# Turning the planes of the normalized rows by transposing DMAs from SBUF to SBUF

## The chip, the core and the metric

The kernel runs on one core of one Trainium2 chip. Its time is the device time of one launch in microseconds (us). Before the change three runs took 516.69, 516.65 and 516.27 us; the median is 516.65. A profiled execution of the same kernel took 516.58 us.

The names of the engines: PE is TensorE's matmuls and PEld its weight loads, DVE is VectorE, ACT is ScalarE, POOL is GpSimd, and SP is SyncE, which issues all DMAs here. SBUF is the memory on the core with 128 partitions, PSUM the memory into which PE writes, and DRAM is the chip's main memory.

## The reference

A causal attention over a window of 64 positions is followed by a mixture layer with SoLU and a layer norm:

```python
scores = scale * np.matmul(q, k.transpose(0, 1, 3, 2))      # B, H, S, D = 8, 8, 576, 64
mask = (rel >= 0) & (rel < 64)                              # rel = query - key position
scores = np.where(mask, scores, -1e9)
attn = np.exp(scores - scores.max(-1)); attn = attn / (attn.sum(-1) + 1e-09)
x = (attn @ v).transpose(0, 2, 1, 3).reshape(4608, 512)
h = x @ w_in                                                # 512 x 1024
sm = softmax of h over the row (with 1e-9 in the sum)
solu = h * sm
ln = (solu - mean) / np.sqrt(var + 1e-06) * g_ln
y = ln @ w_out                                              # 1024 x 512, float32
```

## The kernel before, in words

The 4608 tokens are 36 tiles of 128 (NTILE). For each tile the work has these parts, named after the functions that plan them:

- `load` fetches queries and keys (`qk`, L457) and values (`v`, L459). `scores` (PE, L499) and `softmax` (DVE L513 to L552, ACT L536, POOL) make the attention weights `sS`.
- From tile 8 on, POOL copies the 16-bit halves of `sS` into a buffer `raw` (L572); one DMA stores them to DRAM (`pd`, L580) and one transposing DMA brings them back into `raw` turned (L583). There are 28 such tiles. For the first eight tiles PE transposes `sS`.
- `values` (PE, L630) multiplies the turned weights with the values. ACT and DVE split the result into `xH` and `xL` (DVE L641).
- `moe_in` (PE, L669, and L658 for the first three tiles) multiplies with `w_in`, as three passes over high and low parts, into `pH`: 24 matmuls.
- `moe_norm` makes `e`, the normalized rows of 1024 values: a maximum (DVE L684), exponential (ACT L686), the product with h (DVE L689), small statistics on DVE (L692 to L703), a square (ACT L695), a power on POOL (L702), and the normalization (L708, on POOL or DVE).
- `planes` writes each normalized row as two 16-bit floats, a high plane (L736, mostly ACT) and a low plane (L739, mostly DVE; on POOL for the first tiles). The buffer `pl` is 128 x 2 x 1024, f16, 512 KB a tile.
- `turn` brings both planes into `yT`, with the 1024 features across partitions, as 8 groups of 128. This is done by DMA for tiles 1 to 33, 33 in all; the others are transposed by PE.
- `moe_out` (PE, L802) multiplies `yT` with `w_outH` and `w_outL`: 24 matmuls a tile (high x high, high x low, low x high). ACT scales the result to `ot` (L813), and a DMA stores it (L817).

The loop is a software pipeline. In turn t stand, in this order, `turn(t-1)`, `moe_in(t)` with `moe_norm` and `planes`, `values(t+1)`, the attention of a tile some four ahead, and `moe_out(t-3)`.

The weights are prepared within the first tiles. `weight_block(i)` takes raw 64-bit weights (blocks 0 to 3 are `w_in`, 4 to 7 `w_out`): POOL takes the low bits (L364), DVE joins them (L368, L371, L373). `split` then makes the high parts of `w_in` (L427), the low parts `w_8` to `w_11` (L429), and, scaled by `gs_sb`, `w_outH` (L434) and `w_outL` (L436).

What sets the order: each operation goes to a `Plan` with an engine, an estimated cost, what it reads and what it writes. `Plan.order` gives each one a due time by going back from PE's order, and then lists them: of the operations that are ready on the engine that is free first, the one with the earliest due time comes next. A table `HOMES` puts single tasks on engines, and `RINGS` says how many buffers each name has. SP is one queue in this plan. Where the plan foresees PE waiting in the first stage, it puts in filler matmuls on the identity (`pO_filler`, L911). On the chip each engine works through its list in that order and waits for semaphores.

Of the kernel before, what the change touches and what calls it, by code (L numbers as in the profile page):

```python
# [14 lines left out]
U16 = mybir.dt.uint16  # L15
# [5 lines left out]
P = 128  # L21
# [14 lines left out]
FURTHER = 4  # L36

HASTE = 1

LOOSE = 2  # L40
BEHIND = 3
# [45 lines left out]

RINGS = {
# [3 lines left out]
}  # L92

# [1 line left out]
class Plan:  # L95
# [62 lines left out]
    def order(self):  # L158
        n = len(self.ops)
        before = self.edges()  # L160
        after = [[] for _ in range(n)]
        for i, b in enumerate(before):
            for j, whole in b.items():
                after[j].append((i, whole))
        left = [len(b) for b in before]
        topo = [i for i in range(n) if not left[i]]
        for j in topo:
            for i, _ in after[j]:
                left[i] -= 1
                if not left[i]:  # L170
                    topo.append(i)
        assert len(topo) == n, "the rings are too small for this order"

        clock, due = 0, [1e9] * n
        for i, o in enumerate(self.ops):
            if o[0] == "PE":
                due[i] = clock
                clock += 0 if o[6] else o[1]
        for j in reversed(topo):
            for i, whole in after[j]:  # L180
                lat = self.ops[j][5] if self.ops[i][0] != self.ops[j][0] or self.ops[i][0] == "SP" else 0
                due[j] = min(due[j], due[i] - (HASTE * (self.ops[j][1] + lat) if whole else 0))
        left = [len(b) for b in before]
        ready = [0] * n
        free = dict.fromkeys(("PE", "DVE", "ACT", "POOL", "SP"), 0)
        waiting = {e: set() for e in free}
        for i in range(n):
            if not left[i]:
                waiting[self.ops[i][0]].add(i)
        out, moved, shown = [], 0, False  # L190
        while any(waiting.values()):

            begin, e = min(
                (max(free[e], min(ready[i] for i in w)), e) for e, w in waiting.items() if w)
            i = min((i for i in waiting[e] if ready[i] <= begin), key=lambda i: (due[i], i))
            waiting[e].remove(i)
            if e == "PE" and not shown:
                shown = any(k[0] == "pO" for k in self.ops[i][4])
                n = 0 if shown else int((begin - max(free[e], self.FILL_FROM)) * self.FILL // self.FILL_COST)
                if n > 0:  # L200
                    out.append(self.filler(n))
            out.append(self.ops[i][2])
            end = begin + self.ops[i][1]
            free[e] = end
            if e == "SP":
                free[e] = begin + (1900 if self.ops[i][1] == 2600 else 480)
                moved = end = max(moved, begin) + self.ops[i][1]
            for j, whole in after[i]:
                if whole:
                    ready[j] = max(ready[j], end + (self.ops[i][5] if self.ops[j][0] != e or e == "SP" else 0 if e == "PE" else 90))  # L210
                else:
                    ready[j] = max(ready[j], begin)
                left[j] -= 1
                if not left[j]:
                    waiting[self.ops[j][0]].add(j)
        self.span = max(free.values())
        return out
# [3 lines left out]
def tile_window_attention_solu_moe(  # L221
# [17 lines left out]
    nc = tc.nc  # L239
# [4 lines left out]
    DFF = w_in.shape[1] // 2  # L244
# [3 lines left out]
    NF = DFF // P  # L248
# [6 lines left out]
    dr = ctx.enter_context(tc.tile_pool(name="dr", bufs=3, space=bass.MemoryType.DRAM))  # L255
# [33 lines left out]
    for first in (0, None, 1):  # L289
        t = masks[first] = const.tile([P, P], F32, name=f"mask{first}")  # L290
# [27 lines left out]
    plan = Plan(RINGS)  # L318

    def T(tag, n, shape, dtype=F32, pool=None):  # L320

        if (tag, n) not in plan.tiles:
            plan.tiles[tag, n] = (pool or sb).tile(
                shape, dtype, tag=tag, name=f"{tag}_{n}", bufs=RINGS[tag])
        return plan.tiles[tag, n]

    def W32(i):
        return T("w", i, [P, 2, 512])
# [383 lines left out]
    def crosses(t):  # L712

        return BY_DMA[0] <= t < NTILE - BY_DMA[1]

    def PL(t):
        return T("pl", t, [P, 2, DFF], F16)

    def YD(t):
        return T("yd", t, [2 * P, DFF], U16, pool=dr)  # L720

    def YT(t):
        return T("yF" if t < PLAIN_OUT else "yT", t, [P, NF, P])

    def Y(t, k):

        return YT(t).rearrange("p a b -> p (a b)").bitcast(F16).rearrange(
            "p (a k b) -> p a k b", a=NF, k=2)[:, :, k]
# [13 lines left out]
    def turn(t):  # L742
        if not crosses(t):
            return
        plan.dma(P * DFF * 4, lambda: nc.sync.dma_start(
            YD(t).rearrange("(k p) n -> p k n", k=2), PL(t).bitcast(U16)),
            [("pl", t, h) for h in range(2)] + [("pl", t, h, 1) for h in range(2)], [("yd", t)], 3500)
        plan.op("SP", 2600, lambda: nc.sync.dma_start_transpose(
            YT(t).rearrange("p a b -> p (a b)").bitcast(U16).rearrange("p (a b) -> p a b", a=NF), YD(t)),
            [("yd", t)], [("yT", t)], 2000)  # L750

    def moe_transpose(t):
        if crosses(t):
# [27 lines left out]
    def moe_out(t):  # L781
        last = t == NTILE - 1
        bank = ("pX", NTILE) if last else ("pO", t)

        def PO():
            if last:
                return T(*bank, [P, NC, P], pool=ps_x).rearrange("p a b -> p (a b)")
            return T(*bank, [P, DM], pool=ps_o)

        if t < PLAIN_OUT:  # L790
            for f in range(NF):
                plan.op("PE", 930, lambda f=f: nc.tensor.matmul(  # L792
                    PO(), YT(t)[:, f], W32(NC + f // 2)[:, f % 2],
                    start=(f == 0), stop=(f == NF - 1)),
                    [("yF", t, f), ("w", NC + f // 2)], [bank])
        for f in range(NF if t >= PLAIN_OUT else 0):
            i, x = NC + f // 2, f % 2
            high, low = ([("yT", t)],) * 2 if crosses(t) else (
                [("yT", t, f // 4)], [("yT", t, f // 4, 1)])
            for k, (y, w, keys) in enumerate((  # L800
                    (0, WH, high + [("H", i, x)]), (0, WL, high + [("L", i, x)]), (1, WH, low + [("H", i, x)]))):
                plan.op("PE", 216, lambda f=f, i=i, x=x, k=k, y=y, w=w: nc.tensor.matmul(  # L802
                    PO(), Y(t, y)[:, f], w(i, x), start=(f == k == 0), stop=(f == NF - 1 and k == 2)),
                    keys, [bank])

        def ot():
            return T("ot", t, [P, DM])

        parts = ((slice(0, DM // 2), "ACT", 330), (slice(DM // 2, DM), "DVE", 350)) if last else (
            (slice(0, DM), "ACT", 580),)  # L810
        for x, (cs, e, cost) in enumerate(parts):
            by = 1 / Y_SCALE if t < PLAIN_OUT else unscale
            plan.op(e, cost, lambda cs=cs, e=e, by=by: nc.scalar.mul(  # L813
                ot()[:, cs], PO()[:, cs], by) if e == "ACT" else nc.vector.tensor_scalar(
                ot()[:, cs], PO()[:, cs], by, 0.0, ALU.mult, ALU.add),
                [bank] + [("inv",)] * (t >= PLAIN_OUT), [("ot", t, x)])
            plan.dma(P * DM * 4 // len(parts), lambda cs=cs: nc.sync.dma_start(  # L817
                out[t * P:(t + 1) * P, cs], ot()[:, cs]), [("ot", t, x)], [])
# [43 lines left out]
    for t in range(NTILE + BEHIND):  # L862
        for a in ahead(t):
            on(load, a + 1)
        on(turn, t - 1)
        if t == PLAIN_IN:
            for i in range(NC):
# [13 lines left out]
        else:  # L881
# [16 lines left out]
            if t - BEHIND + 1 >= NTILE - BY_DMA[1]:  # L898
                on(moe_transpose, t - BEHIND + 1)
            on(moe_out, t - BEHIND)  # L900
            if (t, 1) == SCALED:
                out_scale()
# [58 lines left out]
```

## Time and profile before

| what | value |
|---|---|
| median of three runs | 516.65 us |
| profiled execution, whole | 516.58 us |
| its span, first to last instruction | 514.8 us |
| mean granted TensorE clock | 0.996 |
| DMA traffic | 115.57 MB, mean 225 GB/s |
| stores of the planes `yd<-pl` | 33 of 512 KB |
| transposes `yT<-yd` | 33 |

The profile gives busy time by engine, the chain of work that ended last, groups of instructions by line, and rows of a timeline. A row of the chain has start, length and work, all in us. A row of the timeline has start, busy length, engine, line, operation, result and sources by the program's names, shapes and a count; brackets hold the idle time ahead of it and what ended that. A row of the DMA issues has the count, the KB of each and the median us from issue to landing. A row for a stretch of time has its length and the busy time of PE, PEld, DVE, ACT and POOL with counts, the granted clock, the busy share of the DMA engines, and GB/s.

### The profile page before, as it was taken

Reading aid. Unit: us, or ns where it says so; the run is one execution under the profiler, and the core shown is the slowest. Engines: PE = TensorE matmul, PEld = TensorE weight load, DVE = VectorE, ACT = ScalarE, POOL = GpSimd, SP = SyncE. Lnnn points to the kernel's source line nnn. Section 1 sums busy time; section 2 is a strip of 40 time slices with the busy share of each in tenths; the row PEclk is TensorE's granted clock in tenths of the full one; section 3 lists DMA queues with packets and bytes.
Section 4 is the critical chain, followed back from the end, with each engine's and each line's share of the span. In section 5 each row is a group of like instructions: output and inputs, shape, how many; then the busy total and the mean of one; then the engine's idle time right before and its main releaser. Section 6 shows DMA issues by size and latency. Waiting matters only on the chain.

```text
span 514.8 us, 11432 instructions
## 1 busy us (share of the span) xinstructions
PE 503.9 (98%) x4222; PEld 335.7 (65%) x4222; DVE 362.6 (70%) x677; ACT 338.9 (66%) x978; POOL 261.7 (51%) x459
## 2 busy tenths in 40 slices
PE   8899799999999999999999999999999999999997
PEld 7555576666666666666666666666666666666653
DVE  4999997987666777777777777777777777754330
ACT  5577777768866666666666666666666666673240
POOL 5726662457366555555555555555555555571110
PEclk9999999999999999999999999999999999999999
DMA  8992124769899999999999999999999997799201
GB/s 347 415 373 73 52 55 140 212 188 255 234 245 269 260 230 307 253 239 227 272 230 275 235 259 278 268 254 243 253 243 249 295 270 213 183 216 202 85 36 47
DMA packets 157448, 115.57 MB, mean 225 GB/s; under 512 B 129872, under 2 KB 130128, under 8 KB 156880
## 3 DMA queue, kind: packets, MB, share of 16 engines
q1 hardware_dynamic: 157392, 114.84, 81.9%
q8 instruction: 33, 0.54, 0.4%
q14 instruction: 23, 0.19, 0.1%
HBM read 41.42 MB, written 41.42 MB: 161 GB/s over the span
## 4 chain that ended last, share of the span: by engine, by line
PE 90%; DVE 7%; DMA 1%; issue 1%; ACT 1%; DVEq 0%; ACTq 0%
PE pH L669 36%; PE pO L802 35%; PE pX L630 7%; PE pS L499 6%; PE pH L658 2%; DVE w L371 1%; PE pO L792 1%; DVE w L373 1%; DVE w L368 1%; PE pX L802 1%; DVE sS L552 1%; PE t L606 1%; DMA qk<-qk 1%; DVE nmx L520 1%; PE t L764 1%
## 5 line engine op out<-in xcount | busy, mean ns | idle before, releaser
L802 PE MATMUL pO<-w_outH,yT 128*128 128x512 f16 x544 | 167.7, 380 | 0.0
L802 PEld LDWEIGHTS <-yT 128*128 128x128 f16 x840 | 79.6, 98 | 96.6 <-issue 5.1
L552 POOL TENSOR_SCALAR sS<-sS,rec 128x128 f32<-128x128 f32 x240 | 92.4, 406 | 69.1 <-DVE rec L548 64.8
L669 PE MATMUL pH<-w_inH,xH 128*128 128x512 f32 x264 | 111.0, 421 | 3.3 <-DVE mst L689 3.3
L536 ACT ACTIVATE sS<-sS,nmx 128x128 f32<-128x128 f32 x264 | 102.0, 388 | 6.4 <-DVE nmx L513 4.7
L669 PE MATMUL pH<-w_inH,xL 128*128 128x512 f32 x264 | 104.3, 395 | 0.0
L802 PE MATMUL pO<-w_outL,yT 128*128 128x512 f16 x272 | 103.1, 379 | 0.0
L669 PE MATMUL pH<-w,xH 128*128 128x512 f32 x264 | 101.6, 389 | 0.0
L702 POOL TENSOR_TENSOR mst<-mst,neghalf 128x1 f32<-128x1 f32 x36 | 20.8, 579 | 132.0 <-DVE mst L700 130.0
L684 DVE TENSOR_REDUCE mst<-pH 128x1 f32<-128x1024 f32 x36 | 44.0, 1224 | 56.9 <-PE pH L669 55.8
L739 DVE TENSOR_TENSOR pl<-e,pl 128x512 f16<-128x512 f32 x59 | 78.2, 1328 | 3.4 <-ACT pl L736 3.3
L813 ACT ACTIVATE ot<-pO,bound 128x512 f32<-128x512 f32 x34 | 23.4, 688 | 80.1 <-PE pO L802 71.1
L686 ACT ACTIVATE e<-pH,mst 128x1024 f32<-128x1024 f32 x36 | 40.1, 1114 | 32.4 <-DVE mst L684 30.5
L669 PEld LDWEIGHTS pH<-w_inH,xH 128*128 128x128 f32 x264 | 50.2, 190 | 16.1 <-ACT w_inH L427 3.4
L708 POOL TENSOR_SCALAR e<-e,mst 128x512 f32<-128x512 f32 x66 | 51.0, 781 | 18.3 <-DVE mst L703 16.3
L669 PEld LDWEIGHTS pH<-w_inH,xL 128*128 128x128 f32 x264 | 49.9, 189 | 11.9 <-DVE xL L641 0.3
L669 PEld LDWEIGHTS pH<-w,xH 128*128 128x128 f32 x264 | 49.7, 188 | 10.3
L572 POOL COPY raw<-sS 128x1024 uint16<-128x1024 uint16 x52 | 53.0, 1049 | 0.9 <-DVE sS L552 0.9
L695 ACT ACTIVATE unread<-e,mst 128x1024 bf16<-128x1024 f32 x36 | 41.3, 1149 | 16.5 <-DVE mst L693 11.9
L536 ACT ACTIVATION_READ_ACCUMULATOR sS<-sS,nmx 128x1 f32 x264 | 49.6, 188 | 0.0
L689 DVE CUSTOM_DVE_ANT_0 e<-pH,e 128x1024 f32<-128x1024 f32 x36 | 43.8, 1216 | 2.5 <-ACT e L686 2.5
L499 PE MATMUL pS<-qk 64*64 64x128 f32 x1152 | 39.8, 276 | 0.1
(117 smaller groups left out, 706.9 us busy)
## 6 DMA issues: line engine op xcount, KB each, us to landing
qk<-qk SPq DMA_DIRECT2D x36, 640.0 KB, 6.4
yd<-pl SPq DMA_DIRECT2D x33, 512.0 KB, 5.8
pd<-raw SPq DMA_DIRECT2D x28, 512.0 KB, 7.2
v<-vS SPq DMA_DIRECT2D x36, 256.0 KB, 3.6
y<-ot SPq DMA_DIRECT2D x35, 256.0 KB, 6.8
raw<-w_in SPq DMA_DIRECT2D x4, 1024.0 KB, 10.7
raw<-w_out SPq DMA_DIRECT2D x4, 1024.0 KB, 9.0
yT<-yd SPq DMA_TRANSPOSE x33, 5.4
```

Source lines behind the costliest of these rows:

```text
L499: nc.tensor.matmul(PS(t)[half * WIN:(half + 1) * WIN, r, p], q[rs, p, half * WIN:(half + 1) * WIN], keys, start=t not in MASKED, stop=t no ...
L536: plan.op("ACT", 580, lambda h=h: nc.scalar.activation(SS(t)[:, h], PS(t)[:, h // NPAIR, h % NPAIR] if t in MASKED else SS(t)[:, h], AF.Ex ...
L552: SS(t)[:, h], SS(t)[:, h], rec()[:, h:h + 1]) if e == "ACT" else units[e].tensor_scalar(
L572: plan.op(e, {"POOL": 1050, "ACT": 1000, "DVE": 700}[e], lambda x=x, e=e: copy_on(e)(PP(t)[:, :, 4 * x:4 * x + 4].rearrange("p k h n -> p ...
L669: plan.op("PE", 233, lambda n=n, c=c, x=x, w=w: nc.tensor.matmul(PH(t)[:, hs], x(t)[:, c], w(c, h), start=(n == 0), stop=(n == len(passes) ...
L684: plan.op("DVE", 1230, lambda: nc.vector.tensor_reduce(nmax(), PH(t), axis=AX.X, op=ALU.max, negate=True), [("pH", t)], [key(0)])
L686: plan.op("ACT", 1320, lambda: nc.scalar.activation(E(t), PH(t), AF.Exp, bias=nmax(), scale=1.0, accum_out=se()), [("pH", t), key(0)], H2 ...
L689: plan.op("DVE", 1310, lambda: nc.vector.tensor_tensor_reduce(E(t), PH(t), E(t), scale=1.0, scalar=0.0, op0=ALU.mult, op1=ALU.add, accum_o ...
L695: plan.op("ACT", 1330, lambda: nc.scalar.activation(unread, E(t), AF.Square, bias=nmean(), scale=1.0, accum_out=ss()), H2 + [key(4)], [key ...
L708: plan.op(e, {"POOL": 820, "DVE": 400}[e], lambda h=h, hs=hs, e=e: units[e].tensor_scalar(E(t)[:, hs], E(t)[:, hs], nmean(), kk(), ALU.add ...
L739: plan.op(e, {"POOL": 1450, "DVE": 690}[e], lambda hs=hs, e=e: units[e].tensor_sub(PL(t)[:, 1, hs], E(t)[:, hs], PL(t)[:, 0, hs]), [("e", ...
L802: plan.op("PE", 216, lambda f=f, i=i, x=x, k=k, y=y, w=w: nc.tensor.matmul(PO(), Y(t, y)[:, f], w(i, x), start=(f == k == 0), stop=(f == N ...
```

## The change

`turn` no longer stores the planes to DRAM. It issues two transposing DMAs, one for each plane, which read `pl` in SBUF and write every second 128-column group of `yT`. The DRAM buffer `yd` is gone. Each plane has its own key: the first DMA needs the high plane alone, and in `moe_out` the matmuls with the low plane wait for the second DMA. In the plan a plane's DMA has the cost TURN, and SP is held for 1000 ns by it.

```diff
@@ -36,6 +36,7 @@
 FURTHER = 4
 
 HASTE = 1
+TURN = 1400
 
 LOOSE = 2
 BEHIND = 3
@@ -87,7 +88,7 @@
 
 RINGS = {
     "raw": 4, "w": 9, "qk": 3, "v": 4, "vx": 2, "sS": 3, "pd": 3, "PT": 2, "xH": 2, "xL": 2,
-    "e": 3, "pl": 2, "yd": 4, "yF": 1, "yT": 3, "ot": 2, "nmx": 4, "sm": 4, "rec": 4, "mst": 6,
+    "e": 3, "pl": 2, "yF": 1, "yT": 3, "ot": 2, "nmx": 4, "sm": 4, "rec": 4, "mst": 6,
     "pS": 1, "pH": 1, "t": 2, "pX": 1, "pO": 1,
 }
 
@@ -203,7 +204,7 @@
             end = begin + self.ops[i][1]
             free[e] = end
             if e == "SP":
-                free[e] = begin + (1900 if self.ops[i][1] == 2600 else 480)
+                free[e] = begin + {2600: 1900, TURN: 1000}.get(self.ops[i][1], 480)
                 moved = end = max(moved, begin) + self.ops[i][1]
             for j, whole in after[i]:
                 if whole:
@@ -716,9 +717,6 @@
     def PL(t):
         return T("pl", t, [P, 2, DFF], F16)
 
-    def YD(t):
-        return T("yd", t, [2 * P, DFF], U16, pool=dr)
-
     def YT(t):
         return T("yF" if t < PLAIN_OUT else "yT", t, [P, NF, P])
 
@@ -742,12 +740,11 @@
     def turn(t):
         if not crosses(t):
             return
-        plan.dma(P * DFF * 4, lambda: nc.sync.dma_start(
-            YD(t).rearrange("(k p) n -> p k n", k=2), PL(t).bitcast(U16)),
-            [("pl", t, h) for h in range(2)] + [("pl", t, h, 1) for h in range(2)], [("yd", t)], 3500)
-        plan.op("SP", 2600, lambda: nc.sync.dma_start_transpose(
-            YT(t).rearrange("p a b -> p (a b)").bitcast(U16).rearrange("p (a b) -> p a b", a=NF), YD(t)),
-            [("yd", t)], [("yT", t)], 2000)
+        for k in range(2):
+            plan.op("SP", TURN, lambda k=k: nc.sync.dma_start_transpose(
+                YT(t).rearrange("p a b -> p (a b)").bitcast(U16).rearrange(
+                    "p (a k b) -> p a k b", a=NF, k=2)[:, :, k], PL(t)[:, k].bitcast(U16)),
+                [("pl", t, h) if k == 0 else ("pl", t, h, 1) for h in range(2)], [("yT", t, k)], 2000)
 
     def moe_transpose(t):
         if crosses(t):
@@ -795,7 +792,7 @@
                     [("yF", t, f), ("w", NC + f // 2)], [bank])
         for f in range(NF if t >= PLAIN_OUT else 0):
             i, x = NC + f // 2, f % 2
-            high, low = ([("yT", t)],) * 2 if crosses(t) else (
+            high, low = ([("yT", t, 0)], [("yT", t, 1)]) if crosses(t) else (
                 [("yT", t, f // 4)], [("yT", t, f // 4, 1)])
             for k, (y, w, keys) in enumerate((
                     (0, WH, high + [("H", i, x)]), (0, WL, high + [("L", i, x)]), (1, WH, low + [("H", i, x)]))):
```

The due times and SP's free times change with it, and so the plan lists the other engines' work in another order in some places. On POOL, around the low bits of the weight blocks 6 and 7 (`raw_6`, `raw_7`), the low parts of `w_in` (`w_10`, `w_11`) and the power of tile 0 (`mst_0`), the rows before:

```order
L427 CAST w_inH_114<-w_3_356 128x512
L364 TENSOR_SCALAR raw_6_378<-raw_6_378 128x1024
L364 TENSOR_SCALAR raw_7_411<-raw_7_411 128x1024
L429 TENSOR_TENSOR w_10_709<-w_2_313,w_inH_114 128x512
L702 TENSOR_TENSOR mst_0_431<-mst_0_431,neghalf_118 128x1
L429 TENSOR_TENSOR w_11_751<-w_3_356,w_inH_114 128x512
L466 COPY vx_5_758<-v_4_348 64x512
```

and the same place after, where the line numbers are larger by one:

```order
L428 CAST w_inH_114<-w_3_356 128x512
L365 TENSOR_SCALAR raw_6_378<-raw_6_378 128x1024
L430 TENSOR_TENSOR w_10_685<-w_2_313,w_inH_114 128x512
L365 TENSOR_SCALAR raw_7_411<-raw_7_411 128x1024
L430 TENSOR_TENSOR w_11_745<-w_3_356,w_inH_114 128x512
L703 TENSOR_TENSOR mst_0_431<-mst_0_431,neghalf_118 128x1
L467 COPY vx_5_756<-v_4_348 64x512
```

The low bits of block 7 went behind the low part `w_10`, and the power of tile 0 behind `w_11`. On DVE the two small steps L692 and L693 of tile 1 went from there to behind the joins of blocks 6 and 7. In the same way POOL's low plane of tile 1 (`pl_1`, L739) went from ahead of tile 2's power (`mst_2`, L702) to behind it.

On PE one filler group is gone. Between the values of tile 4 and the scores of tile 6, before:

```order
L630 MATMUL pX_4_849<-PT_4_813,vx_4_772 64x64 x2
L630 MATMUL pX_4_849<-PT_4_813,v_4_348 64x64 x2
L911 MATMUL pO_filler_174<-ident_81 128x128
L499 MATMUL pS_6_882<-qk_6_462 64x128 x16
L792 MATMUL pO_0_913<-w_4_509,yF_0_869 128x512 x2
```

and after:

```order
L631 MATMUL pX_4_845<-PT_4_811,vx_4_770 64x64 x2
L631 MATMUL pX_4_845<-PT_4_811,v_4_348 64x64 x2
L500 MATMUL pS_6_870<-qk_6_462 64x128 x16
L789 MATMUL pO_0_902<-w_4_509,yF_0_862 128x512 x2
L789 MATMUL pO_0_902<-w_5_516,yF_0_862 128x512 x2
```

The rest of PE's order stays. On SP, one tile of the steady state, before:

```order
L459 DMA v_17_2356<-vS 128x512
L748 DMA_TRANSPOSE yT_10_2363<-yd_10_2263 128x8x256
L583 DMA_TRANSPOSE raw_14_132<-pd_14_2280 128x8x256
L457 DMA qk_19_2403<-qk 128x1280
L745 DMA yd_11_2414<-pl_11_2354 128x2x1024
L580 DMA pd_15_2431<-raw_15_133 128x2048
L817 DMA y<-ot_9_2422 128x512
```

and after:

```order
L581 DMA pd_15_2410<-raw_15_133 128x2048
L814 DMA y<-ot_9_2406 128x512
L744 DMA_TRANSPOSE yT_11_2443<-pl_11_2428 128x8x128 x2
L584 DMA_TRANSPOSE raw_15_133<-pd_15_2410 128x8x256
L458 DMA qk_20_2505<-qk 128x1280
L460 DMA v_18_2512<-vS 128x512
```

Before, a pair of planes was stored, and turned one tile later. After, the pair is turned where the store stood, behind the stores of `pd` and `y`.

## The prediction

> **What bounds the kernel now.** First the page's head and the share of its chain by engine:
>
> ```profile
> span 514.8 us, 11432 instructions
> PE 503.9 (98%) x4222; PEld 335.7 (65%) x4222; DVE 362.6 (70%) x677; ACT 338.9 (66%) x978; POOL 261.7 (51%) x459
> PE 90%; DVE 7%; DMA 1%; issue 1%; ACT 1%; DVEq 0%; ACTq 0%
> ```
>
> PE is busy for 98% of the span, and 90% of the chain that ended last is PE. The chain of waits, read in order of time, shows where the rest lies. First around the start of the steady state, then one whole tile of it:
>
> ```profile
> 61.96 1.13 DVE e L689
> 63.12 0.14 issue
> 63.25 4.64 PE pH L669 x12
> ...
> 73.53 0.42 PE pO_filler L911 x2
> ...
> 97.09 2.95 PE pH L669 x12
> ...
> 240.98 5.50 PE pH L669 x24
> 246.48 1.08 PE pX L630 x32
> 247.56 1.03 PE pS L499 x32
> 248.59 5.29 PE pO L802 x24
> 253.88 5.50 PE pH L669 x24
> ```
>
> From 240.98 every step starts where the last one ended: a tile is 5.50 + 1.08 + 1.03 + 5.29 = 12.90 us of PE. No DMA stands in it. The last step that isn't PE is DVE's h·e product of tile 2 (L689), behind which PE starts tile 3 at 63.25. The stretches say the same (columns: length, PE, PEld, DVE, ACT, POOL with counts, clock, DMA share, GB/s):
>
> ```profile
> 0.00:63.25 63.25, 56.00 (x530) 38.63 (x531) 54.72 (x102) 41.69 (x123) 35.62 (x65) 1.00 0.65 256
> 130.00:440.00 310.00, 310.00 (x2692) 207.66 (x2692) 218.16 (x385) 213.88 (x628) 170.01 (x308) 1.00 0.98 253
> 248.80:254.00 5.20, 5.20 (x26) 2.54 (x25) 5.20 (x6) 2.38 (x7) 4.48 (x10) 1.00 0.98 205
> 254.00:261.00 7.00, 7.00 (x79) 5.70 (x81) 3.32 (x11) 5.76 (x21) 2.08 (x3) 1.00 1.00 308
> ```
>
> From 130 to 440 us PE has no idle time, so a DMA that arrives sooner there gains nothing. Yet the DMA engines are busy for 0.98 of it: they are the rail that this change could hit. Before 63.25 DVE is busy for 54.72 of 63.25 us, and what it does late is paid.
>
> **The change part by part.** Removed: 33 stores of 512 KB; 33 transposes of a pair of planes become 66 of one plane.
>
> ```profile
> yd<-pl SPq DMA_DIRECT2D x33, 512.0 KB, 5.8
> pd<-raw SPq DMA_DIRECT2D x28, 512.0 KB, 7.2
> raw<-pd SPq DMA_TRANSPOSE x28, 4.8
> 248.61 2.48 SPq L748 DMA_TRANSPOSE yT<-yd  x1
> 251.20 2.18 SPq L583 DMA_TRANSPOSE raw<-pd  x1
> 254.42 0.39 SPq L745 DMA_DIRECT2D yd<-pl  x1
> 254.87 0.45 SPq L580 DMA_DIRECT2D pd<-raw  x1
> ...
> 259.38 1.08 PE pX L630 x32
> ```
>
> DMA time per tile. The two transposes of a tile (yT and raw, 512 KB each) are issued at 248.61 and 251.20, and the DMA engines run them in the 5.20 us from 248.80 to 254.00: 2.6 us each. The other 7.00 us of the period carry 308 GB/s, about 2.16 MB, so the store's 512 KB are 1.7 us. Afterwards raw's transpose (2.6) and the other transfers (7.0 − 1.7 = 5.3) take 7.9 of 12.9 us, and 5.0 is left for two plane transposes. At half of the row of 2.6 they are 1.3 each, 2.6 together, and the rail has 2.4 us to spare. Their source is SBUF, which no row shows. From below, 0.8 each at the plain transfers' 308 GB/s; from above, the whole 2.6 each, if cost goes by instruction, which makes 5.2 and overruns by about 0.2 us a tile. I take 1.3, nearest in operation and bytes. On PE's chain: 0.
>
> SP's queue. Per tile it loses 0.39 and a 2.48 and gains two holds, between half of 2.48 and 2.48 each: at most 2.1 us more. Nothing on PE's chain is that close behind it. The wait is the old one: the store waited at its place for tile t's planes (issued 254.42), and now the pair waits for them, the first one for the high plane alone. Behind the pair stand raw's transpose, qk and v, and so an overdue plane would hold these three. Before, the pair of planes stored at 254.42 was turned one period later (248.61 + 12.90 = 261.51), landed within 5.2 us and was read 12.9 us after its issue, at 259.38 + 1.08 + 1.03 = 261.49 for the one shown. The new pair needs no landed store and can be issued some 7 us sooner. Raw's transpose, read by the values' product (L630), lands at 251.20 + 4.8 = 256.0, which is 3.4 us ahead of 259.38; its own store, issued at 254.87, lands at 262.1, still ahead of that transpose's old place in the next period (251.20 + 12.90 = 264.10), so that the pair ahead of it costs nothing while the planes take under 2 us more. I take 0 for the queue; the cover is this slack of 2 to 3.4 us for raw and over 7 for yT. If it were gone, each tile would wait for raw at L630, and SP's 2.1 us would be the most that is paid. That end belongs to the same case as slow transposes (rival 4).
>
> The filler. PE's order is the same except for one filler group ahead of tile 6's scores, the 0.42 at 73.53 on the chain. Gone: −0.42; it is 0 if the scores wait as long anyway. I take −0.42, since the chain shows no other engine there.
>
> The reorder in the ramp, the largest term. The planner, fed with other costs for SP, also orders POOL's and DVE's work around 58 us anew. The rows of both engines there, the wait that they end in, and the shape of the moved instruction (fewest, mean and most ns):
>
> ```profile
> 63.25 0.76 PE L669 MATMUL pH<-w_inH,xH 128*128 128x512 f32 x1 [3.28 <-DVE mst L689]
> 52.16 3.42 POOL L364 TENSOR_SCALAR raw<-raw 128x1024 int32<-128x1024 uint32 x2
> 58.32 1.27 POOL L429 TENSOR_TENSOR w<-w,w_inH 128x512 fp32r<-128x512 f32 x1 [2.74 <-DVE w L429]
> 60.60 0.60 POOL L702 TENSOR_TENSOR mst<-mst,neghalf 128x1 f32<-128x1 f32 x1 [1.01 <-DVE mst L700]
> 61.16 1.33 POOL L429 TENSOR_TENSOR w<-w,w_inH 128x512 fp32r<-128x512 f32 x1
> 48.53 3.07 DVE L552 TENSOR_SCALAR sS<-sS,rec 128x128 f32<-128x128 f32 x4
> 54.46 0.14 DVE L692 TENSOR_SCALAR mst<-mst 128x1 f32<-128x1 f32 x1
> 59.20 0.93 DVE L429 TENSOR_TENSOR w<-w,w_inH 128x512 fp32r<-128x512 f32 x1
> 60.49 0.88 DVE L552 TENSOR_SCALAR sS<-sS,rec 128x128 f32<-128x128 f32 x4
> L364 POOL TENSOR_SCALAR raw<-raw x7: 1137/1555/2040, 8.8 to 53.5; 128x1024 int32<-128x1024 uint32 x7
> ```
>
> PE idles 3.28 us before 63.25, waiting for DVE. DVE's four multiplies at 60.49 take 0.88 beside POOL's tiny power; the same four at 48.53 took 3.07 beside POOL's large L429. Before, POOL did both halves of the low bits (L364, raw_6 and raw_7) at 52.16, then stood idle for 1.01 us ahead of 60.60. Now raw_7's L364 stands behind w_10's L429, and w_11's L429 follows it ahead of the power. So from 58.3 POOL works: w_10 until 59.5; L364 lasts 1.14 to 2.04 us, here behind DVE's L429 (ending at 60.0), so until about 61.05; w_11's 1.33, until about 62.4. DVE's multiplies, ready at 60.49, now stand beside two large POOL instructions. If they get through only as POOL ends, they start 62.4 − 60.49 = 1.9 later; some 0.1 comes back in the gaps: +1.8. From above, 3.07 − 0.88 = 2.19 and 0.1 for their neighbours: +2.3. From below, DVE has two tiny instructions of tile 1 less before 57 us (L692, L693), and if POOL's work hides, the start is earlier by one such length: −0.14. I take +1.8; the row at 48.53 is the same instruction beside the same neighbour. All PE work behind 63.25 moves with it.
>
> Tile 1's low plane. POOL computes it at 74.92 in 2.27 us, now behind tile 2's power, at about 84 to 86:
>
> ```profile
> 74.92 2.27 POOL L739 TENSOR_TENSOR pl<-e,pl 128x512 f16<-128x512 f32 x2
> 85.07 4.40 DVE L436 SCALAR_TENSOR_TENSOR w_outL<-w,gs_sb,w_outH 128x512 f16<-128x512 f32 x6
> 95.41 0.68 DVE L641 TENSOR_TENSOR xL<-pX,xH 128x512 fp32r<-128x512 f32 x1
> ```
>
> There DVE's L436 runs. DVE's next due result is xL at 95.41 + 0.68 = 96.09, read at 97.09: 1.0 us of slack. Of 2.27 blocked, 1.27 would reach PE; it lies on both sides of other gaps, so I take +0.2 (bounds 0 and 1.3).
>
> Sum: +1.8 − 0.42 + 0.2 = +1.6. The profiled execution took 516.58 (span 514.8), 0.07 under the median of 516.65, and its 1.8 us outside the span stay: 516.58 + 1.6 = **518.2**.
>
> The clock is weighed here:
>
> ```profile
> 63.25:66.67 3.42, 3.42 (x8) 2.59 (x9) 3.42 (x7) 2.21 (x5) 2.59 (x3) 0.50 0.31 77
> 66.67:70.00 3.33, 3.33 (x20) 2.81 (x19) 3.33 (x6) 2.18 (x10) 0.00 (x0) 1.00 0.00 0
> ```
>
> Behind the pause of 3.28 us PE ran at half clock for 3.42 us, and so lost 1.71. In the sum that loss moves along unchanged with the later start. If instead the return to full clock stays at its place in time, the later start (63.25 + 1.8 = 65.05) has 1.62 us of half clock, loses 0.81, and 0.90 is won: 517.3. If so short a stretch is not enough, half clock lasts 3.42 us more, to 70.09, loses 2.52, and 0.81 is added: 519.0. The Trainium skill, "TensorE: Matmul & The Clock Gate", Part 1, says that the gate watches windows of about 3.4 us which run free of the kernel. That rule would give one of the last two; the trace's 3.42 agrees on the window's length, but one pause cannot show what the window is counted from.
>
> **The rivals.**
> 1. The clock's return is fixed in time, as worked out: 517.3 or 519.0. For it: 3.42 us at exactly half. Against: the start at half clock and the end of the pause coincide.
> 2. POOL's and DVE's work interleaves and nothing reaches PE but the missing filler: 516.58 − 0.14 − 0.42 = 516.0. For it: POOL had 1.01 idle. Against: the row at 48.53.
> 3. Faster, by the clock: the start comes 0.14 earlier, the pause is 3.14, and from some length between the two on the clock is not lowered. That wins 1.71 + 0.14 + 0.42: 514.3. It decides only if POOL's work hides; no shorter pause is seen here.
> 4. Transposes out of SBUF are slow. Above 2.5 us each the DMA engines overrun the 12.9 us; at 3.4 each by about 1.8 us on each of some 27 tiles: 565. With the 2.6 from above: 522. For it: no row. Against: bytes halve.
>
> **How the numbers follow.** Forecast 0.40 (own range 517.4 to 519.4); rival 1, 0.12; rival 2, 0.27; rival 3, 0.12; rival 4, 0.09. About 0.2%, 1.0 us, is what can be told from no change. Faster: rival 3, 0.12. Same: rival 2, half of rival 1, and 0.05 of the forecast below 517.7: 0.38. Slower: the rest, 0.50. The range goes from 514.2 (rival 3) to 519.8 (rival 1's end, and the ramp at its bounds), and leaves out rival 4.
>
> **What would show it.** Right: PE's L669 of tile 3 starts near 65 behind DVE L689, with a pause near 5 us; DVE's four multiplies ahead of it take 2 us or more beside POOL; a tile is still 12.90 us with PE idle 0 from 130 to 440; each plane's transpose near 1.3 us. Wrong: a start at 63.2 or before, a row of clock 1.00 right behind the pause, or a PE wait for yT.

## The result, and the profile after

| | us | runs |
|---|---|---|
| before, beside this comparison | 516.46 median, 516.23 to 516.69 | 4 |
| after | 520.89 median, 520.36 to 521.03 | 4 |
| ratio | 1.0084, interval 1.0066 to 1.0101 | |
| profiled execution, before and after | 516.58 and 520.36 | |

The change makes the kernel 4.4 us slower. The prediction was 518.2, with a range that ended at 519.8: the direction was right, the time lies outside.

The page of the kernel after, its span and busy times, the DMA queue, the shares of the chain, and the two transposing DMAs (count, median us from issue to landing):

```profile
span 518.5 us, 11407 instructions
PE 505.6 (97%) x4220; PEld 336.0 (65%) x4220; DVE 342.4 (66%) x677; ACT 337.6 (65%) x978; POOL 253.3 (49%) x459
q1 hardware_dynamic: 149472, 97.54, 68.7%
PE 86%; DVE 9%; DMA 2%; ACT 1%; issue 1%; SPq 0%; DVEq 0%; ACTq 0%
yT<-pl SPq DMA_TRANSPOSE x66, 2.8
raw<-pd SPq DMA_TRANSPOSE x28, 4.9
```

A q1 line has packets, MB and the share of the engines' time. DVE's share of the chain rose from 7% to 9%, and this queue moves 97.54 MB instead of 114.84. Next the steady state as a stretch (length; PE, PEld, DVE, ACT, POOL; clock, DMA share, GB/s), SP's issues of one tile, and one step of the chain:

```profile
130.00:440.00 310.00, 310.00 (x2692) 207.89 (x2691) 196.51 (x385) 212.32 (x629) 166.80 (x314) 1.00 0.82 213
...
248.05 2.76 SPq L744 DMA_TRANSPOSE yT<-pl  x2
251.22 2.79 SPq L584 DMA_TRANSPOSE raw<-pd  x1
...
244.73 5.50 PE pH L670 x24
```

The steady state is as it was: PE has no idle time, and moe_in takes 5.50 us. The DMA engines are busy for 0.82 of the time instead of 0.98. The step that began at 240.98 before begins at 244.73 now, 3.75 us later. At the end the distance is the same (the last scaling starts at 511.26 and 515.01). So the whole loss is made before that, in the first stage. These are PE's places where it comes in, and the end of the DVE product in front of the first of them:

```profile
63.55 1.21 DVE L690 CUSTOM_DVE_ANT_0 e<-pH,e 128x1024 f32<-128x1024 f32 x1
64.91 0.76 PE L670 MATMUL pH<-w_inH,xH 128*128 128x512 f32 x1 [4.90 <-ACT vx L467]
...
75.17 1.03 PE pS L500 x32
76.20 7.06 PE pO L789 x16
...
93.67 0.38 PE L799 MATMUL pO<-w_outL,yT 128*128 128x512 f16 x1 [0.62 <-DVE w_outL L437]
...
102.30 2.38 PE L607 MATMUL t<-ident,sS 128*128 128x128 f32 x8
104.67 2.75 PE pH L670 x12
```

The kernel before has at these places, beside the 63.25 shown above:

```profile
74.98 7.07 PE pO L792 x16
...
100.05 0.87 PE t L606 x8
100.92 2.76 PE pH L669 x12
```

How late PE is against it:

- Tile 3 starts at 64.91 instead of 63.25: 1.66 late. The bracket names a copy of ACT (`vx`), which ended 0.01 us behind DVE's product (63.55 + 1.21 = 64.76). Before, PE started while ACT was still at these copies (until 63.97), so the product is what PE waits for; in e2_raw7 and e6b_all below the bracket names it.
- Tile 0's moe_out starts at 76.20 instead of 74.98: 1.22 late. The missing filler gave 0.44 back.
- The first moe_out that needs `w_outL` waits 0.62 us for DVE. Behind it PE is about 2.1 late.
- The eight transposes of tile 6's weights take 2.38 us instead of 0.87; they wait inside for the softmax. Behind them PE is 104.67 − 100.92 = 3.75 late, and this stays.

The lists of DVE, ACT and POOL differ in more places than the few shown under the change. One of the others matters below: DVE's cast of tile 2's high plane (L736, now L734) stood behind six of the `w_outL` steps and stands ahead of them now.

### The profile page after: what moved, and what is told of

It reads as the page before. It is cut to its first block, busy times and chain, and to the rows that moved or that the text cites. A ratio compares the mean times of both kernels' runs of the same rounds, so it can differ in the third digit from the quotient of the medians.

```text
span 518.5 us, 11407 instructions
## 1 busy us (share of the span) xinstructions
PE 505.6 (97%) x4220; PEld 336.0 (65%) x4220; DVE 342.4 (66%) x677; ACT 337.6 (65%) x978; POOL 253.3 (49%) x459
## 3 DMA queue, kind: packets, MB, share of 16 engines
q1 hardware_dynamic: 149472, 97.54, 68.7%
## 4 chain that ended last, share of the span: by engine, by line
PE 86%; DVE 9%; DMA 2%; ACT 1%; issue 1%; SPq 0%; DVEq 0%; ACTq 0%
PE pH L670 34%; PE pO L799 34%; PE pX L631 7%; PE pS L500 6%; DMA raw<-w_in 2%; PE pH L659 2%; DVE w_outL L437 1%; PE pO L789 1%; DVE w L372 1%; PE pX L799 1%; PE t L607 1%; DVE w L374 1%; DVE w L369 1%; DVE mst L685 1%; PE t L761 1%
## 5 line engine op out<-in xcount | busy, mean ns | idle before, releaser
L553 POOL TENSOR_SCALAR sS<-sS,rec 128x128 f32<-128x128 f32 x240 | 85.6, 378 | 154.6 <-DVE rec L549 80.2
L537 ACT ACTIVATE sS<-sS,nmx 128x128 f32<-128x128 f32 x264 | 103.2, 394 | 75.7 <-DVE nmx L533 70.3
L737 DVE TENSOR_TENSOR pl<-e,pl 128x512 f16<-128x512 f32 x59 | 41.8, 710 | 64.6 <-ACT pl L734 63.1
L467 ACT COPY vx<-v 64x512 f32<-64x512 f32 x63 | 38.9, 617 | 0.4
## 6 DMA issues: line engine op xcount, KB each, us to landing
raw<-w_in SPq DMA_DIRECT2D x4, 1024.0 KB, 10.6
```

What stands on the lines that cost most here:

```text
L537: plan.op("ACT", 580, lambda h=h: nc.scalar.activation(SS(t)[:, h], PS(t)[:, h // NPAIR, h % NPAIR] if t in MASKED else SS(t)[:, h], AF.Ex ...
L553: SS(t)[:, h], SS(t)[:, h], rec()[:, h:h + 1]) if e == "ACT" else units[e].tensor_scalar(
L737: plan.op(e, {"POOL": 1450, "DVE": 690}[e], lambda hs=hs, e=e: units[e].tensor_sub(PL(t)[:, 1, hs], E(t)[:, hs], PL(t)[:, 0, hs]), [("e", ...
```

## The experiments

All but e10_before_fill start from the changed kernel. "Moved" means that an engine's list is rearranged after the plan has made it; nothing else of the list changes. Ratios are to the kernel before, run beside each experiment. There its medians were 516.92 to 516.95, against 516.46 beside the change, and the changed kernel was not run again. So a gain that is counted from 520.89 can be some 0.5 us too small; where it matters, the gain counted against the kernel before stands in brackets.

### e5_due: one number, so that the old order comes back

```diff
-                [("pl", t, h) if k == 0 else ("pl", t, h, 1) for h in range(2)], [("yT", t, k)], 2000)
+                [("pl", t, h) if k == 0 else ("pl", t, h, 1) for h in range(2)], [("yT", t, k)], 8830)
```

> The changed kernel with one number changed: the latency that the plan adds behind a plane's transpose is 8830 instead of 2000, so that the due times of all work ahead of it are what they were with the store. PE, DVE, ACT and POOL then work in the order of the kernel before, and only SP's queue and the two DMAs are those of the change. If the whole loss of 4.4 us comes from the order of the other engines: 516.5 us, as before (within 0.5), with PE's moe_in of tile 3 starting near 63.2. If the transposes out of SBUF themselves cost time: it stays at or near 520.9.

Measured: 516.81, ratio 0.9994 (0.9982 to 1.0007). With this number PE, DVE, ACT and POOL have the rows of the kernel before, every one; SP's queue and the DMAs are the new ones. PE starts tile 3 at 63.14. So the two transposes out of SBUF cost nothing and bring nothing, within the interval (0.9 us less to 0.4 us more), and the 4.4 us are the order.

It also says where the order comes from. Before, the plan put 1542 + 3500 + 150 (store) and 2600 + 2000 + 150 (transpose) between a plane and moe_out: 9942 ns. After, 1400 + 2000 + 150 = 3550. So every step that makes a plane is due 6.4 us later, and comes behind other work. With 8392, which makes the sums equal, POOL's order at raw_7 still stayed as in the changed kernel; the low plane is read two matmuls (432 ns) into moe_out, which the old single key did not know, and 8830 covers both and gives the old order.

### e2_raw7: POOL's low bits of block 7 back

```diff
+    plan.moves = [
+        (("POOL", ("raw", 7)), ("POOL", ("raw", 6))),
+    ]
```

Each entry names an instruction and the one behind which it is put.

> The changed kernel with one instruction moved back: POOL's low bits of weight block 7 stand behind those of block 6 again, ahead of the low part w_10. If POOL's work beside DVE's four multiplies is what moved the start of tile 3: the start comes back from 64.9 to about 63.3, and the time falls by 1.6 to about 519.2, with the later stalls as they are. If DVE is late there for another reason: 520.9.

Measured: 520.22, ratio 1.0056 (1.0043 to 1.0069): 0.7 (1.2) of the 1.6 us expected. The timelines of POOL and DVE, of the changed kernel first:

```profile
59.60 1.41 POOL L365 TENSOR_SCALAR raw<-raw 128x1024 int32<-128x1024 uint32 x1
61.09 1.26 POOL L430 TENSOR_TENSOR w<-w,w_inH 128x512 fp32r<-128x512 f32 x1
59.98 1.05 DVE L546 TENSOR_SCALAR rec<-sm 128x8 f32<-128x8 f32 x1
61.30 1.72 DVE L553 TENSOR_SCALAR sS<-sS,rec 128x128 f32<-128x128 f32 x4
```

and of e2_raw7:

```profile
60.21 1.27 POOL L453 TENSOR_TENSOR w<-w,w_inH 128x512 fp32r<-128x512 f32 x1 [0.72 <-DVE rec L569]
59.96 0.16 DVE L569 TENSOR_SCALAR rec<-sm 128x8 f32<-128x8 f32 x1
60.39 1.75 DVE L576 TENSOR_SCALAR sS<-sS,rec 128x128 f32<-128x128 f32 x4
64.03 0.47 PE L693 MATMUL pH<-w_inH,xH 128*128 128x512 f32 x1 [4.02 <-DVE mst L713]
```

The late start has two halves. POOL's low bits hold a DVE instruction of 0.16 us for 1.05: 0.89, and this half is gone here (64.91 to 64.03). The other half is w_11's low part, which stands ahead of tile 0's power in the new order too, beside DVE's four multiplies: 1.72 or 1.75 instead of 0.88. Of the 0.9 us gained here, 0.65 are left at tile 6's transposes (101.65 against 102.30).

### e3_stats and e3b_stats: tile 1's normalization and planes back

Both put DVE's small steps of tile 1, ACT's square and casts, and POOL's normalization and low planes at their old places. They differ in one anchor, the instruction behind which tile 1's power is put (− in e3_stats, + in e3b_stats):

```diff
-        (("POOL", ("mst", 1, 5)), ("POOL", ("vx", 5, 1))),
+        (("POOL", ("mst", 1, 5)), ("POOL", ("vx", 5, 0))),
```

> The changed kernel with tile 1's normalization and planes (DVE's and POOL's small steps, ACT's square and casts, POOL's two low planes) back at their old places. If POOL's low plane of tile 1 at 84 us beside DVE is what makes DVE late for w_outL, xL and the reciprocal of tile 6: the two stalls between 92 and 104 us (2.5 us) go, 518.4. If the stall at tile 6's transposes comes from the order of DVE's own steps: only 0.8 to 1.2 goes, about 519.9. If POOL does not matter there: 520.9.

Measured: 523.12, ratio 1.0115 (1.0102 to 1.0128), slower than the change. The anchor was the wrong copy: tile 1's power and its normalization stood ahead of the second half of w_11, which waited with them. The row of PE:

```profile
75.73 0.80 PE L693 MATMUL pH<-w,xH 128*128 128x512 f32 x1 [2.65 <-POOL w L453]
```

This run says nothing on the question; it shows that POOL's lateness there reaches PE (2.65 us).

> The same edit as e3_stats, but with tile 1's power on POOL behind the second half of w_11, so that nothing of w_11 is held up. If POOL's low plane of tile 1 at 84 us makes DVE late: w_outL, xL and the reciprocal of tile 6 are on time, PE's stalls between 92 and 104 us (2.5 us) go, and the time is 518.4. If the stall at tile 6's transposes (1.3 us) comes from the order of DVE's own steps, 519.7. If neither: 520.9.

Measured: 519.28, ratio 1.0043 (1.0031 to 1.0056): 1.6 (2.1) of the 2.5 us. The list of PE's waits in this stage, its transposes of tile 6 in the chain, and DVE's w_outL; then POOL and DVE at that place in the changed kernel:

```profile
PE pH L693 <- ACT vx L490: 5.0, 1, 5.0
102.05 1.56 PE t L630 x8
86.83 7.05 DVE L460 SCALAR_TENSOR_TENSOR w_outL<-w,gs_sb,w_outH 128x512 f16<-128x512 f32 x7
```

```profile
83.99 2.29 POOL L737 TENSOR_TENSOR pl<-e,pl 128x512 f16<-128x512 f32 x2
86.41 2.05 POOL L435 TENSOR_SCALAR w_outH<-w,gs_sb 128x512 f16<-128x512 f32 x2
89.44 1.60 POOL L737 TENSOR_TENSOR pl<-e,pl 128x512 f16<-128x512 f32 x1
84.11 1.05 DVE L704 SCALAR_TENSOR_TENSOR mst<-mst 128x1 f32<-128x1 f32 x1
85.09 1.22 DVE L405 TENSOR_SCALAR gs_sb<-g_sb,bound 128x8 f32<-128x8 f32 x1
87.91 7.04 DVE L437 SCALAR_TENSOR_TENSOR w_outL<-w,gs_sb,w_outH 128x512 f16<-128x512 f32 x7
```

In the changed kernel tile 1's low plane holds two tiny DVE steps for about a us each (1.05, and 1.22 instead of 0.23 for gs_sb), so DVE begins w_outL 4.6 us behind the end of moe_out(0) (87.91 against 83.27) instead of 3.0 (85.07 against 82.05). e3b_stats takes this away: DVE begins w_outL 2.8 us behind the end of moe_out(0) (86.83 against 84.03), and the wait for w_outL is gone. Many steps of tile 1 were moved at once; that the low plane is the one that counts is read from these rows and was not run alone.

What stays is a stall of 1.56 − 0.87 = 0.7 us at tile 6's transposes. The w_outL steps are as slow here as in the changed kernel, 7.05 us for seven, about 1.0 each, against 4.40 for six before, 0.73 each. So their slowness does not come from tile 1. Before, POOL stood idle there and waited for DVE's cast of tile 2, which came behind six w_outL steps; now the cast comes first, and POOL's low plane of tile 2 (L737 at 89.44 above) runs beside w_outL. The rows of the kernel before, then the cast of the changed one:

```profile
89.39 0.41 DVE L736 CAST pl<-e 128x512 f16<-128x512 f32 x1
89.89 1.16 POOL L739 TENSOR_TENSOR pl<-e,pl 128x512 f16<-128x512 f32 x1 [3.62 <-DVE pl L736]
87.58 0.41 DVE L734 CAST pl<-e 128x512 f16<-128x512 f32 x1
```

That this cast is the cause of the last 0.7 us is argued; no run moved it.

### e4_rec: the reciprocal of tile 6 ahead of the maximum of tile 7

```diff
+        (("DVE", ("nmx", 7, 0)), ("DVE", ("rec", 6), 1)),
+        (("ACT", ("sS", 6, 0), 1), ("ACT", ("mst", 3, 3))),
...
```

The lines left out put the other seven heads behind this one.

> The changed kernel with DVE's maximum of tile 7 behind the reciprocal of tile 6, and ACT's scaling of tile 6 ahead of the output scaling of tile 1, as they stood before. If the stall at tile 6's transposes (1.34 us) comes from this order: it falls by about 1.2 to 519.7. If it comes from DVE being late as a whole: at most 0.3 falls, 520.6.

Measured: 520.69, ratio 1.0067 (1.0055 to 1.0079): 0.2 (0.7). The profiled execution, at the same mean clock as that of the changed kernel, took 520.17 against 520.36. The transposes are shorter, and a later step waits instead:

```profile
102.24 1.32 PE L630 MATMUL t<-ident,sS 128*128 128x128 f32 x8
107.19 0.27 PE L654 MATMUL pX<-PT,vx 128*64 128x64 f32 x1 [0.59 <-DVE PT L635]
```

DVE is late as a whole; which of these two steps comes first mostly chooses who waits.

### e6b_all: the three places together

The moves of e2_raw7 and e3b_stats, and

```diff
+        (("POOL", ("mst", 0, 5)), ("POOL", ("w", 10, 0))),
```

This line puts tile 0's power ahead of w_11.

> The changed kernel with three moves: POOL's low bits of block 7 ahead of w_10, POOL's power of tile 0 ahead of w_11, and tile 1's steps as in e3b_stats. The rest of the changed order, and the missing filler, stay. If these three places are the whole loss: PE starts tile 3 at 63.2 and has no stall behind it, so 0.4 under the kernel before for the filler: 516.3. If the e2 result of 0.9 us (of 1.7) is all that POOL's order is worth: about 517.5. If the loss sits elsewhere in the new order: 519 or more.

Measured: 517.14, ratio 1.0005 (0.9996 to 1.0013). PE's first row of tile 3:

```profile
63.11 0.48 PE L693 MATMUL pH<-w_inH,xH 128*128 128x512 f32 x1 [3.27 <-DVE mst L713]
```

With e3b_stats alone the wait there was still 5.0 us, so POOL's order at 58 to 62 us is the whole of the late start (the power's move was not run alone). The three places hold all but 0.2 to 0.3 us of the loss. That fits the stall of 0.7 us at tile 6 that remains (101.27 − 99.70 = 1.57 instead of 0.87) less 0.4 for the filler.

### e7_fill, e8_fill_after, e10_before_fill: the pause and the clock

Filler matmuls ahead of tile 3's moe_in, 6 in the plan, are made 18 (e7_fill: with e5_due's number; e10_before_fill: the kernel before) or 24 (e8_fill_after: the changed kernel):

```diff
+    plan.fills = {("PE", ("pH", 3)): 18}
```

> The kernel of e5_due (the order of before, the new DMAs) with 18 filler matmuls instead of 6 ahead of tile 3's moe_in, so that PE is busy until about 63.2 us and does not pause for 3.3 us. If the pause is what lowers the clock: 1.00 behind it in every run, 1.7 us less than 516.6, so 514.9, and the runs lie within 0.5 us of each other instead of three groups 1.3 us apart. If the clock depends on something else: 516.8 as e5_due, with the same groups.

> The changed kernel with 24 filler matmuls instead of 6 at the same place, which fills its pause of 4.9 us. If the longer pause costs it a longer stretch of half clock in most runs: 1.7 to 2.3 us less than 520.9, so 518.6 to 519.2, in one group. If the clock is no part of the loss: 520.9 less the same 1.7 us as e7_fill wins, so 519.2, and no narrower groups. If the clock depends on something else than the pause: 520.9.

> The kernel before, with its store and its transposing DMA out of DRAM, and the 18 filler matmuls of e7_fill instead of 6. If the new DMAs buy nothing, as PE never waited for the old ones: 515.4, the same as e7_fill. If they help somewhere once the pause is filled: slower than e7_fill, 515.8 or more.

| kernel | us, all runs | ratio to before |
|---|---|---|
| e7_fill | 515.41 (515.25 to 515.67) | 0.9969 (0.9958 to 0.9981) |
| e10_before_fill | 515.35 (515.16 to 515.58) | 0.9970 (0.9960 to 0.9981) |
| e8_fill_after | 519.62 (519.55 to 519.83) | 1.0050 (1.0037 to 1.0064) |

The stretches show the clock behind the pause (the column ahead of the DMA share). First the changed kernel, profiled in its run of 520.36:

```profile
64.91:68.00 3.09, 3.09 (x7) 2.35 (x8) 3.09 (x7) 0.06 (x1) 2.35 (x3) 0.50 0.33 85
68.00:72.00 4.00, 4.00 (x22) 3.32 (x22) 4.00 (x4) 3.43 (x16) 0.38 (x1) 0.96 0.00 0
```

then e3b_stats, which has the same pause, profiled with a mean clock of 0.993:

```profile
68.50:70.00 1.50, 1.50 (x5) 1.17 (x4) 1.50 (x3) 0.93 (x6) 0.00 (x0) 0.50 0.00 0
70.00:72.00 2.00, 2.00 (x15) 1.73 (x14) 2.00 (x5) 1.20 (x3) 0.00 (x0) 0.99 0.00 0
```

and e7_fill, with its one wait of PE in this stage:

```profile
63.72:67.00 3.28, 3.28 (x17) 2.75 (x18) 3.28 (x6) 2.06 (x7) 2.08 (x3) 1.00 0.30 80
PE pH L693 <- DVE mst L713: 0.6, 1, 0.6
```

The half clock ends soon after 68 in the first, at about 70 in the second, and does not appear in the third, where PE waits 0.6 us instead of 3.3. With the pause filled, all runs of a kernel lie within 0.5 us. Without, the runs of the kernel before that stood beside the experiments fall into groups by their mean granted clock: 515.4 at 0.999, 516.4 to 517.4 at 0.996 to 0.997, 517.6 to 518.4 at 0.993, apart from single runs in between. So a pause of PE of 3.3 us costs nothing, about 1.4 or about 2.5 us in different runs of one program.

The traces also show that the low clock is not tied to the end of the pause. These are e3b_stats while PE still pauses, and e6b_all behind PE's start at 63.11:

```profile
63.00:64.00 1.00, 0.00 (x0) 0.00 (x0) 1.00 (x2) 1.00 (x3) 0.52 (x1) 0.60 0.00 0
63.00:64.00 1.00, 0.86 (x3) 0.53 (x4) 1.00 (x3) 0.96 (x3) 0.17 (x2) 1.00 0.00 0
64.00:65.00 1.00, 1.00 (x5) 0.78 (x4) 1.00 (x3) 1.00 (x2) 1.00 (x2) 0.68 0.33 23
```

Worked out from such rows, half clock lasts from 63.2 to 70.0 in e3b_stats (mean clock 0.993), 6.8 us, and begins 1.7 us before PE does. In e5_due's profile (0.993) it lasts from 62.6 to 69.5. In e6b_all (0.996) it lasts from 64.4 to 67.8, 3.4 us, and begins 1.3 us behind PE's start. So it comes in stretches of 3.4 or 6.8 us that may begin on either side of PE's start, and in the kernel before they coincide by chance.

The longer pause of the changed kernel (4.9) had 0.993 in three of its four runs (520.79 to 521.03) and 0.997 in the profiled one. So of the 4.4 us between the medians 3.8 are in the two profiles, which have nearly the same mean clock. With both pauses filled the two orders stand 519.62 − 515.41 = 4.2 us apart. The order alone costs nearly all of the loss, whatever the clock does; how much of the rest is clock, from 0.2 to 0.6 us, is not settled. e8_fill_after came out above the 518.6 to 519.2 that was expected. Its profile shows why: from 54.6 to 101.8 us its chain is DVE's, with a few steps of POOL and ACT and none of PE, and so tile 6's transposes start at 101.79, only 0.5 us earlier than without the filler.

e10_before_fill equals e7_fill within 0.1 us, so the new DMAs help nowhere; both beat the two kernels of the change. e7_fill wins 1.5 us; 1.7 were expected.

### e9_twice: what a transpose out of SBUF costs the DMA engines

```diff
+            def twice(k=k):
+                for to in (YT(t), T("again", t, [P, NF, P])):
...
+            plan.op("SP", TURN, twice,
```

> The kernel of e5_due with each plane's transpose issued twice, the second time into a buffer that nobody reads: 66 transposes more. The changed kernel's DMA engines were busy for 0.82 of the 12.90 us of a tile, 10.6 us. If a plane's transpose out of SBUF costs them 1.33 us, two more make 13.2 to 13.3 us, more than the tile has: 0.3 to 0.4 us on each of some 27 tiles, so 525 to 528. If it costs only 0.8: 12.2 us, still hidden, 516.8. If it costs 2.6 as the two-plane one did: over 560.

Measured: 528.34, ratio 1.0227 (1.0205 to 1.0249). Its steady state and PE's wait:

```profile
130.00:440.00 310.00, 300.81 (x2618) 201.33 (x2620) 205.93 (x371) 205.18 (x601) 165.56 (x295) 0.99 1.07 244
PE pX L631 <- DMA raw<-pd: 9.1, 10, 2.6
```

The time lies just above the 525 to 528 that stood for 1.33 us a plane. PE is idle for 9.2 of 310 us, waiting for raw's transpose, which queues behind the others. A tile then takes 12.90 × 310 / 300.81 = 13.3 us. If the DMA engines are what is full, a plane of 256 KB takes (13.3 − 10.6) / 2 = 1.35 us of all of them; with the share of 0.86 in e5_due's own profile, 11.1 us, it is 1.1. This is an estimate. The share is no strict limit: in one tile of the changed kernel (142.9 to 155.8 us) it is 1.10, and PE does not wait. SP's queue is full here too: from 300 to 327 us it issues without a pause, and raw's transpose holds it for 3.9 and 5.1 us, against a median of 2.0 in the changed kernel. The run does not tell the two apart.

## Why the prediction was right or wrong

- **What bounds the kernel: right.** PE's steady state did not move by 0.01 us a tile, and the reorder in the ramp decided the sign.
- **DMA time, 1.3 us a plane: right as far as it shows.** The share of 0.82 is 10.6 us of 12.90, where the sum had 7.9 + 2.6 = 10.5; e9_twice gives 1.1 to 1.35. (256 KB at 308 GB/s are 0.85, not 0.8.) Rival 4 is out: PE waits for no DMA behind 60 us. Weight loads for moe_out waited for yT in nine places, 1.5 us in all, and PE had no idle time by it. SP's hold is 1.26 us a plane at the median, near the half of 2.48 that was the lower bound.
- **The filler, −0.42: right** (1.66 to 1.22).
- **The late start of tile 3, +1.8: right (1.66), the size in part by luck.** The mechanism was half named: the row at 48.53 stood for the multiplies beside L429, which cost 0.85 us; the other 0.89 is a tiny step ahead of the reciprocal (L546) that waits for the whole of POOL's low bits. e2_raw7 and e6b_all show the two halves. The row at 48.53 was no firm price either: the same four multiplies, beside the same work of POOL, take 1.95 us instead of 3.07 in the changed kernel's profile. Rival 2 (all hidden) and rival 3 are out.
- **Tile 1's low plane, +0.2 with 1.3 as its end: the step that failed.** PE loses 2.5 us there (1.22 to 3.75). The term set POOL's 2.27 us against the slack of one result, xL, beside DVE's w_outL steps. In the run the low plane comes ahead of them: it holds two tiny steps, one of which makes the `gs_sb` that w_outL reads, for 0.9 and 1.0 us, so that w_outL itself is late, and then tile 6's softmax. e3b_stats shows 1.6 to 2.1 us to come from tile 1's steps. The remaining stall of 0.7 us was in no term: w_outL takes 7.04 + 0.73 us for its eight steps instead of 4.40 + 1.75, with tile 1's steps in either place. That this comes from tile 2's cast and low plane is only argued. With 2.5 in place of 0.2 the sum is 1.66 − 0.44 + 2.5 = 3.7, and the profiled execution is 3.8 slower.
- **The clock (rival 1): the loss moved along in the profiled pair, by chance.** Half clock lasts 3.42 us before and about 3.4 after (64.91 to 68.3), as the sum took it. But that it began with PE's start, which spoke against rival 1, is not so in other profiles. The rule of the Trainium skill ("TensorE: Matmul & The Clock Gate", Part 1), windows of about 3.4 us that run free of the kernel, agrees with the stretches of 3.4 and 6.8 us and with the groups in which runs of one program fall. The groups are 0.9 to 1.5 us apart, less than the 1.71 that a whole window at half clock would cost PE; part of the longer stretch falls into the pause (0.5 us in e5_due's profile), and that does not account for all of it. The sum took one profile's clock for the kernel's, and with the longer pause most runs came out one group lower. The range also took rival 1's end and the ramp's bounds one at a time; together they would have ended at about 520.3, still under the 520.9 measured.

## What to carry to other kernels

Where a list scheduler orders the engines, a cheaper transfer changes the due times of all work ahead of it. Compare the engines' orders as a whole, and if they differ, give the plan back the old latency, to see transfer and order apart. When a large step of one engine moves beside another engine that it slows, ask which tiny steps it will hold and who reads them, and not only when the next large result is due. A pause of TensorE like the one of 3.3 us here is worth filling with matmuls that nobody reads: that gave 1.5 us and made the runs agree, while the change of DMAs gave nothing.

## What the runs showed of the hardware that was not expected

- One POOL instruction holds a DVE instruction of 0.15 to 0.23 us for 0.9 to 1.0 us more (0.16 to 1.05, 0.15 to 1.05, 0.23 to 1.22), so that tiny steps beside POOL are the dear ones. The Trainium skill ("SBUF — State Buffer", Who interferes with whom) says that a DVE instruction in a mode with two ports contends with GpSimd: the one that issues first has the shared pair of ports for its whole instruction, and the other one blocks. The rows agree with the blocking: the held steps end at 59.98 + 1.05 = 61.03 and 85.09 + 1.22 = 86.31, and POOL's work ends at 59.60 + 1.41 = 61.01 and 83.99 + 2.29 = 86.28. Which mode these steps use, no run here shows.
- A transpose of 256 KB out of SBUF lands in 2.8 us at the median and holds SP for 1.26 us; 512 KB out of DRAM took 5.4 and 2.6. Half the bytes cost about half; the source differs too, and no run here changes one without the other.
- The same program with a pause of 3.3 us on TensorE has three times, 515.4, about 516.8 and about 517.9 us, which go with mean granted clocks of 0.999, 0.996 to 0.997 and 0.993. In the profiles of this case the low clock comes in stretches of 3.4 or 6.8 us, which begin from 1.7 us before the end of the pause (e3b_stats) to 1.3 us behind it (e6b_all).
